# Entering the second part of three programs in the first instructions of a decode attention kernel

## The chip, the cores and the metric

The kernel runs on one core of a Trainium2 chip. A core has five engines that run programs of their own: TensorE (PE, matrix products; its weight loads are shown as PEld), VectorE (DVE), ScalarE (ACT), GpSimd (POOL) and SyncE (SP). Engines wait for one another through semaphores. Data moves between the chip's main memory (HBM) and the core's working memory (SBUF) by transfers that 16 DMA engines carry out; the engines' own program code is fetched by the same DMA engines, on queues that the profile calls "instruction". The metric is the device time of one execution in microseconds (us).

## The reference

One decode step of attention, 16 heads, one query row for each, 8192 keys of 256 numbers, all in bf16:

```python
B, H, Sq, Sk, D = 1, 16, 1, 8192, 256
scale = q.shape[-1] ** -0.5
scores = jnp.einsum("bhqd,bhkd->bhqk", q, k) * scale
p = _softmax(scores, axis=-1)
return jnp.einsum("bhqk,bhkd->bhqd", p, v)
```

K and V are 67 MB each and each of their numbers is used once.

## The kernel before, in words

The program of each engine is written out by hand; no scheduler moves anything. The keys of a head lie as 128 partitions of 64 keys, so a head's K is a buffer of 128 x 16384 bf16 numbers (4.19 MB) and its 64 columns of 256 numbers each hold 128 keys. There are two K buffers and two V buffers, used by even and odd heads.

**SP** (line 136) issues all K and V transfers in one order, the list `stream` of line 57: the first 16 columns of K of head 0, the other 48, K of head 1, half of V of head 0, K of head 2, the other half of V of head 0, half of V of head 1, and so on, with K two heads ahead of V. K of head h waits until VectorE and TensorE are done with head h-2 in that buffer (lines 132, 133), V until the weighted sum of head h-2 is done (line 135). All transfers go through one queue.

**DVE** computes the scores of the first 48 columns of a head: one multiply-and-sum for each column (line 189, two instructions), then the maximum over the head's 64 columns (line 206). It runs a loop of eight turns with an even and an odd head in each; the loop is one body of 213 instructions.

**PE** computes the other 16 columns: it transposes four K columns at a time (`ktrans`, line 278), ACT copies the result to SBUF (`evac`, line 367), and PE multiplies by q (`kscore`, line 292). It also combines the maximum across partitions (lines 226, 232), and makes the weighted sum of V (`pv`, line 257, 64 matmuls a head). Before its loop it spreads q over the partitions (lines 314 to 338). Its loop has nine turns: turn i computes the scores of heads 2i and 2i+1 and the weighted sums of heads 2i-2 and 2i-1, in the order scores, `pv`, scores, `pv`; turn 0 has no `pv` and turn 8 no scores, and conditional branches step over those parts.

**ACT** issues the load of q (line 401), copies the spread q out of PSUM (lines 404, 412), copies the q of the next head (line 362), evacuates the transposes, makes the exponentials (line 379), scales and stores the output rows (lines 392, 399).

What orders the work around the change is the programs' own order. DVE's program is 220 instructions as written, ACT's 83, PE's 599, with a matmul counted as two. DVE's loop begins at its instruction 4, ACT's loop at its instruction 18, PE's loop at its instruction 41.

Of the kernel before, what the change touches and what calls it, by code (L numbers as in the profile page):

```python
# [15 lines left out]
V_LATE = {14: (0, 16, 32, 48), 15: (0, 16, 32, 44, 52, 58, 62)}  # L16
AHEAD = {"kd": 1, "sc": 1, "sp": 2, "ex": 2, "m": 1, "g": 1, "mT": 1, "l": 1, "bc": 1, "nb": 1, "rc": 2, "pv": 2, "fin": 4}
V_SEMS = (("va0", "v0b", "v0c", "v0d"), ("va1", "v1b", "v1c", "v1d", "v1e", "v1f", "v1g"))
# [22 lines left out]
def bass_standalone__mha_softmax__decode_kernel(nc: bass.Bass, q: bass.AP, k: bass.AP, v: bass.AP, out: bass.AP):  # L41
    B, H, Sq, D = q.shape
    Sk = k.shape[2]
    P = 128
    J = Sk // P
    NH = D // P
# [24 lines left out]
    with contextlib.ExitStack() as ctx:  # L71
# [9 lines left out]
        def sem(name):  # L81
            if name not in sems:
                sems[name] = ctx.enter_context(nc.semaphore(name))
            return sems[name]
# [3 lines left out]
        q_sb = sb("q_sb", [H, D], dt)  # L88
# [5 lines left out]
        m = sb("m", [P, 2], FP32)  # L94
        g = sb("g", [1, 2], FP32)
# [4 lines left out]
        identb = sb("identb", [P, P], BF16)  # L100
# [8 lines left out]
        sm = ps("sm", [P, 512])  # L109
        qps = ps("qps", [P, 512])  # L110

        for name in ("pool", "cb", "cf", "qp", "qs", "qb", "kd", "tp", "kt", "sp", "sc", "m", "mT", "g", "bc", "nb", "ex"):
            sem(name)
        for name in ("l", "rc", "pv", "fin", "ldq", "k0", "k0b", "k1", "va0", "va1", "v1h", "o0", "o1"):
            sem(name)
# [1 line left out]
        for row in V_SEMS:  # L117
            for name in row[1:]:
                sem(name)

        def src(t, h):
            return t[0, h].rearrange("(p j) d -> p (j d)", p=P)

        if True:
# [44 lines left out]
            @(lambda f: f(nc.vector))  # L169
            def _(dve):  # L170
                def xmax(h):
                    dve.wait_ge(sem("mT"), h.of(1, 2))
                    dve.tensor_reduce(g[0:1, h.par : h.par + 1], mx[0:1, 0:P], AX.X, ALU.max).then_inc(sem("g"), 1)  # L173

                def recips(h):
                    dve.wait_ge(sem("l"), h.of(1, 2))
                    dve.wait_ge(sem("fin"), h.of(1, 3))
                    dve.reciprocal(recip[0:1, h.par : h.par + 1], qps[0:1, 0:1]).then_inc(sem("rc"), 1)  # L178

                def head(h, at):  # L180
                    dve.wait_ge(sem("qb"), h.of(1, 1))
                    dve.wait_ge(sem("ex"), h.of(1, 1))
                    dve.wait_ge(sem(f"k{h.par}"), h.of(8, 16 - 8 * h.par))
                    buf = kbuf[h.par]
                    for j in range(JD):
                        if j == K_FIRST and h.par == 0:

                            dve.wait_ge(sem("k0b"), 16)
                        ins = dve.tensor_tensor_reduce(  # L189
                            out=buf[:, j * D : (j + 1) * D],  # L190
                            in0=buf[:, j * D : (j + 1) * D],
                            in1=q_now[h.par][:, 0:D],
                            scale=SCALE,
                            scalar=0.0,
                            op0=ALU.mult,
                            op1=ALU.add,
                            accum_out=S[h.par][:, j : j + 1],
                        )
                        if j in at:
                            at[j]()  # L200
                    ins.then_inc(sem("kd"), 1)
                    if JD in at:
                        at[JD]()
                    dve.wait_ge(sem("kd"), h.of(1, 2))
                    dve.wait_ge(sem("sc"), h.of(1, 2))
                    dve.tensor_reduce(m[:, h.par : h.par + 1], S[h.par][:, :], AX.X, ALU.max).then_inc(sem("m"), 1)  # L206

                with dve.Fori(0, H // 2) as i:
                    ev, od = _Step(0, i), _Step(1, i)
                    prev = od.back(2)  # L210

                    def later(f):
                        with dve.If(i > 0):
                            f(prev)

                    head(ev, {40: lambda: later(xmax)})
                    head(od, {2: lambda: later(recips), 3: lambda: xmax(ev), JD: lambda: recips(ev)})
                last = _Step(H - 1)
                xmax(last)
                recips(last)  # L220

            @(lambda f: f(nc.tensor))
            def _(pe):
                def transpose_m(h):
                    pe.wait_ge(sem("m"), h.of(1, 2))
                    pe.matmul(  # L226
                        mx[0:1, 0:P], lhsT=m[:, h.par : h.par + 1], rhs=ident[:, :], start=True, stop=True
                    ).then_inc(sem("mT"), 1)
# [21 lines left out]
                def pv(h, waits, at):  # L250

                    pe.wait_ge(sem("fin"), h.of(1, 3))
                    pe.wait_ge(sem(f"va{h.par}"), h.of(8, 32 - 8 * h.par))
                    for j in range(J):
                        for name, value in waits.get(j, ()):
                            pe.wait_ge(sem(name), value)
                        ins = pe.matmul(  # L257
                            acc[h.par][0:1, 0:D],
                            lhsT=E[h.par][:, j : j + 1],
                            rhs=vbuf[h.par][:, j * D : (j + 1) * D],  # L260
                            start=(j == 0),
                            stop=(j == J - 1),
                        )
                        if j == J - 1:
                            ins.then_inc(sem("pv"), 1)
                        if j + 1 in at:
                            at[j + 1]()
# [33 lines left out]
                def scores(t, before=None):  # L301
                    if before:
                        transpose_m(before)
                    for gi in range(NG):
                        ktrans(t, gi)
                        if gi >= 1:
                            kscore(t, gi - 1)
                        if gi == 1 and before:
                            bcast(before)
                    kscore(t, NG - 1)  # L310
                    if before:
                        total(before)

                pe.wait_ge(sem("ldq"), 16)
                pe.wait_ge(sem("cb"), 1)
                for hf in range(NH):
                    ins = pe.matmul(
                        qps[:, hf * H : (hf + 1) * H],
                        lhsT=q_sb[:, hf * P : (hf + 1) * P],
                        rhs=identb[0:H, 0:H],  # L320
                        start=True,
                        stop=True,
                    )
                ins.then_inc(sem("qp"), 1)
                for h in range(H):
                    pair = h // 2
                    if h % 2 == 0 and pair >= 2:
                        pe.wait_ge(sem("qs"), pair - 1)
                    ins = pe.matmul(  # L329
                        acc[pair % 2][:, (h % 2) * D : (h % 2 + 1) * D],  # L330
                        lhsT=identb[0:H, h : h + 1].to_broadcast([H, P]),
                        rhs=q_sb[:, :],
                        start=True,
                        stop=True,
                    )
                    if h % 2 == 1:
                        ins.then_inc(sem("qp"), 1)
                pe.wait_ge(sem("cf"), 4)
                with pe.Fori(0, H // 2 + 1) as i:
                    ev, od = _Step(0, i), _Step(1, i)  # L340
                    fin_turn = pe.snap((i // 8) * 16 + 16)
                    half_turn = pe.snap(((i + 1) // 8) * 16 + 16)
                    old = od.back(2)
                    with pe.If(i < H // 2):
                        scores(ev)
                    with pe.If(i > 0):
                        pv(
                            ev.back(2),
                            {V_LATE[14][n]: [(V_SEMS[0][n], fin_turn)] for n in range(1, len(V_SEMS[0]))},
                            {32: lambda: transpose_m(old), 48: lambda: bcast(old), 64: lambda: total(old)},  # L350
                        )
                    with pe.If(i < H // 2):
                        scores(od, before=ev)
                    with pe.If(i > 0):
                        waits = {V_LATE[15][n]: [(V_SEMS[1][n], fin_turn)] for n in range(1, len(V_SEMS[1]))}
                        waits[HALF].append(("v1h", half_turn))
                        pv(old, waits, {})

            @(lambda f: f(nc.scalar))
            def _(act):  # L360
# [38 lines left out]
                    act.dma_start(dst, o_sb[h.par][0:1, :]).then_inc(sem(f"o{h.par}"), 16)  # L399

                act.dma_start(q_sb[:, :], q[0, :, 0, :]).then_inc(sem("ldq"), 16)
                by_head = q_all[:, 0 : H * QW].rearrange("p (h w) -> p h w", w=QW)
                act.wait_ge(sem("qp"), 1)
                act.activation(
# [75 lines left out]
```

## Time and profile before

| | |
|---|---|
| median of 3 runs | 320.71 us (320.42 to 320.89) |
| the profiled execution, whole | 321.04 us |
| its span, first to last instruction | 319.6 us |
| busy: DVE, PE, ACT | 274.9, 220.9, 92.0 us |
| moved by DMA | 134.29 MB, 420 GB/s over the span |
| instruction fetches | 5 packets, 0.05 MB |
| mean granted TensorE clock | 0.84 |

The page gives one profiled execution. Its parts are the busy time of each engine, the span in 40 slices with the granted clock and the DMA load, the DMA queues, the chain of work that ended last, the costliest groups of instructions and the DMA issues. Other views are tables of chosen stretches of time (windows), lists of instructions in order of time (timelines), the chain in order of time, and DMA queues within a stretch.

### The profile page before, as it was taken

Reading aid. Unit: us, or ns where it says so; the run is one execution under the profiler, and the core shown is the slowest. Engines: PE = TensorE matmul, PEld = TensorE weight load, DVE = VectorE, ACT = ScalarE, POOL = GpSimd, SP = SyncE. Lnnn points to the kernel's source line nnn. Section 1 sums busy time; section 2 is a strip of 40 time slices with the busy share of each in tenths; the row PEclk is TensorE's granted clock in tenths of the full one; section 3 lists DMA queues with packets and bytes.
Section 4 is the critical chain, followed back from the end, with each engine's and each line's share of the span. In section 5 each row is a group of like instructions: output and inputs, shape, how many; then the busy total and the mean of one; then the engine's idle time right before and its main releaser. Section 6 shows DMA issues by size and latency. Waiting matters only on the chain.

```text
span 319.6 us, 6845 instructions
## 1 busy us (share of the span) xinstructions
PE 220.9 (69%) x2162; PEld 156.3 (49%) x2162; DVE 274.9 (86%) x1584; ACT 92.0 (29%) x171; POOL 1.6 (0%) x11
## 2 busy tenths in 40 slices
PE   4427186797875947849297573966749477397997
PEld 1326154565554635626256352653626355265675
DVE  2799999999999998897979979889797997979910
ACT  5436050433224060510506123060231605116010
POOL 1000000000000000000000000000000000000000
PEclk9999999769598786969769598785969969587799
DMA  8999999999999999999999999999999999999994
GB/s 329 451 397 455 392 453 416 416 427 435 439 418 443 431 435 439 418 439 427 439 435 423 439 418 443 431 431 435 427 439 414 447 435 427 439 406 423 422 399 179
DMA packets 6549, 134.29 MB, mean 420 GB/s; under 512 B 752, under 2 KB 912, under 8 KB 1424
## 3 DMA queue, kind: packets, MB, share of 16 engines
q1 hardware_dynamic: 6480, 134.22, 98.3%
q8 instruction: 2, 0.03, 0.0%
q10 hardware_dynamic: 64, 0.02, 0.0%
q14 instruction: 3, 0.02, 0.0%
HBM read 134.23 MB, written 0.01 MB: 420 GB/s over the span
## 4 chain that ended last, share of the span: by engine, by line
DMA 49%; PE 24%; DVE 23%; issue 2%; ACT 1%; ACTq 0%; SPq 0%; DVEq 0%
DMA vbuf<-in_v_dram 45%; PE acc L257 23%; DVE kbuf L189 22%; DMA kbuf<-in_k_dram 4%; DVE S L189 1%; PE sm L232 1%; ACT KT L367 1%; PE mx L226 0%; ACT o_sb L392 0%; ACT q_now L362 0%; DVE g L173 0%; SPq L136 0%; PE spe L292 0%; ACTq L399 0%; DVE recip L178 0%
## 5 line engine op out<-in xcount | busy, mean ns | idle before, releaser
L189 DVE CUSTOM_DVE_ANT_0 kbuf<-kbuf,q_now 128x256 bf16<-128x256 bf16 x768 | 268.1, 413 | 22.2 <-DMA kbuf<-in_k_dram 21.2
L257 PE MATMUL acc<-vbuf,E 128*1 128x256 bf16 x1024 | 147.6, 315 | 36.3 <-DMA vbuf<-in_v_dram 36.3
L257 PEld LDWEIGHTS acc<-vbuf,E 128*1 128x1 bf16 x1024 | 96.7, 96 | 80.4 <-DMA vbuf<-in_v_dram 37.3
L367 ACT ACTIVATE KT<-tp 128x1024 bf16<-128x1024 bf16 x64 | 63.8, 1018 | 30.3 <-PE tp L278 30.1
L189 DVE DVE_READ_ACCUMULATOR2_ANT S<- 128x1 f32 x768 | 58.4, 76 | 0.0
L278 PE MATMUL tp<-identb,kbuf 128*128 128x128 bf16 x512 | 42.3, 239 | 13.9 <-DMA kbuf<-in_k_dram 13.8
L292 PE MATMUL spe<-q_now,KT 128*128 128x1 bf16 x512 | 23.1, 166 | 32.3 <-ACT KT L367 31.6
L278 PEld LDWEIGHTS tp<-identb,kbuf 128*128 128x128 bf16 x512 | 33.5, 107 | 18.3 <-DMA kbuf<-in_k_dram 12.4
L292 PEld LDWEIGHTS spe<-q_now,KT 128*128 128x128 bf16 x512 | 18.0, 100 | 42.0 <-ACT KT L367 32.0
L392 ACT ACTIVATE o_sb<-acc,recip 1x256 bf16<-1x256 f32 x16 | 7.4, 464 | 99.9 <-PE acc L257 98.6
L375 ACT ACTIVATE negb<-sm 128x1 f32<-128x1 f32 x16 | 2.8, 172 | 84.5 <-PE sm L232 84.5
L173 DVE TENSOR_REDUCE g<-mx 1x1 f32<-1x128 f32 x16 | 4.4, 276 | 9.8 <-PE mx L226 9.8
L226 PE MATMUL mx<-ident,m 128*1 128x128 f32 x32 | 6.3, 279 | 5.7 <-DVE m L206 5.7
L232 PE MATMUL sm<-g,ones_row 1*128 1x1 f32 x32 | 6.2, 262 | 4.1 <-DVE g L173 4.1
L232 PEld LDWEIGHTS sm<-g,ones_row 1*128 1x128 f32 x32 | 4.9, 190 | 6.2 <-DVE g L173 4.7
L362 ACT ACTIVATE q_now<-q_all 128x258 bf16 (+1 forms) x17 | 7.0, 412 | 0.3 <-DVE S L189 0.3
L178 DVE RECIPROCAL recip<-qps 1x1 f32<-1x1 f32 x16 | 2.4, 151 | 3.9 <-PE qps L242 3.9
L379 ACT ACTIVATE E<-S,negb 128x64 bf16<-128x64 f32 x16 | 5.6, 348 | 0.5
L226 PEld LDWEIGHTS mx<-ident,m 128*1 128x1 f32 x32 | 2.2, 83 | 6.3 <-DVE m L206 5.9
L329 PE MATMUL acc<-q_sb,identb 16*128 16x256 bf16 x16 | 4.4, 403 | 1.0 <-ACT q_all L412 1.0
L371 ACT ACTIVATE S<-spe 128x16 f32<-128x16 f32 x16 | 2.9, 183 | 7.3 <-PE spe L292 7.3
L412 ACT ACTIVATE q_all<-acc 128x512 bf16<-128x512 f32 x8 | 4.4, 593 | 0.9 <-PE acc L329 0.9
(20 smaller groups left out, 16.6 us busy)
## 6 DMA issues: line engine op xcount, KB each, us to landing
kbuf<-in_k_dram SPq DMA_DIRECT2D x15, 4096.0 KB, 20.5
vbuf<-in_v_dram SPq DMA_DIRECT2D x11, 4096.0 KB, 29.0
vbuf<-in_v_dram SPq DMA_DIRECT2D x6, 2048.0 KB, 24.4
vbuf<-in_v_dram SPq DMA_DIRECT2D x6, 1024.0 KB, 12.8
kbuf<-in_k_dram SPq DMA_DIRECT2D x1, 3072.0 KB, 11.7
kbuf<-in_k_dram SPq DMA_DIRECT2D x1, 1024.0 KB, 4.8
vbuf<-in_v_dram SPq DMA_DIRECT2D x1, 768.0 KB, 9.1
vbuf<-in_v_dram SPq DMA_DIRECT2D x1, 512.0 KB, 9.9
```

The source lines that it names most:

```text
L173: dve.tensor_reduce(g[0:1, h.par : h.par + 1], mx[0:1, 0:P], AX.X, ALU.max).then_inc(sem("g"), 1)
L189: ins = dve.tensor_tensor_reduce(out=buf[:, j * D : (j + 1) * D], in0=buf[:, j * D : (j + 1) * D], in1=q_now[h.par][:, 0:D], scale=SCALE, ...
L226: pe.matmul(mx[0:1, 0:P], lhsT=m[:, h.par : h.par + 1], rhs=ident[:, :], start=True, stop=True).then_inc(sem("mT"), 1)
L232: pe.matmul(sm[:, 0:1], lhsT=ones_row[0:1, 0:P], rhs=g[0:1, h.par : h.par + 1], start=True, stop=True,).then_inc(sem("bc"), 1)
L257: ins = pe.matmul(acc[h.par][0:1, 0:D], lhsT=E[h.par][:, j : j + 1], rhs=vbuf[h.par][:, j * D : (j + 1) * D], start=(j == 0), stop=(j == J ...
L278: ins = pe.transpose(tp[gi % 2][:, b * D + hf * P : b * D + (hf + 1) * P], buf[:, j * D + hf * P : j * D + (hf + 1) * P], identb[:, :],)
L292: ins = pe.matmul(spe[:, c : c + 1], lhsT=KT[gi % 2][:, b * D + hf * P : b * D + (hf + 1) * P], rhs=q_now[h.par][:, D + hf : D + hf + 1], ...
L329: ins = pe.matmul(acc[pair % 2][:, (h % 2) * D : (h % 2 + 1) * D], lhsT=identb[0:H, h : h + 1].to_broadcast([H, P]), rhs=q_sb[:, :], start ...
L362: act.activation(out=q_now[h.par][:, :], in_=src_q, func=ACT.Copy).then_inc(sem("qb"), 1)
L367: act.activation(out=KT[gi % 2][:, :], in_=tp[gi % 2][:, :], func=ACT.Copy).then_inc(sem("kt"), 1)
L379: act.activation(out=E[h.par][:, :], in_=S[h.par][:, :], func=ACT.Exp, bias=negb[:, h.par : h.par + 1], scale=1.0, accum_out=lsum[:, h.par ...
L392: act.activation(out=o_sb[h.par][0:1, :], in_=acc[h.par][0:1, 0:D], func=ACT.Copy, scale=recip[0:1, h.par : h.par + 1],).then_inc(sem("fin ...
```

## The change: an early visit to later code

TensorE, VectorE and ScalarE each execute, in their first instructions, a jump to code that lies further on in their program. For VectorE and ScalarE a new helper writes an `If` that is never taken around 50 and 66 no-operations, so that the engine jumps over them; the code behind is moved on by as many instructions. VectorE's helper stands ahead of its loop, ScalarE's behind the issue of the q load. For TensorE no padding is used: the first half of the loop's body is put in an inner loop, which has one empty turn (r = 0) in turn 0 of the outer loop, so that the program runs to the inner loop's end and back again; in all other turns of the outer loop the inner one begins at r = 1 and runs once. The spreading of q, formerly ahead of the loop, becomes the first part of that inner body and is done in turn 0. The work, its order on each engine and its waits are the same.

```diff
+        def skip_ahead(eng, n):
+
+            zero = eng.alloc_register(f"zero_{n}_{eng.engine.value}")
+            eng.reg_mov(zero, 0)
+            with eng.If_ne(zero, 0):
+                for _ in range(n):
+                    eng.nop().then_inc(sem("pad"), 1)
...
+                skip_ahead(dve, 50)
                 with dve.Fori(0, H // 2) as i:
...
-                pe.wait_ge(sem("ldq"), 16)
-                pe.wait_ge(sem("cb"), 1)
...
+                def spread_q():
+                    pe.wait_ge(sem("ldq"), 16)
+                    pe.wait_ge(sem("cb"), 1)
...
                 with pe.Fori(0, H // 2 + 1) as i:
...
-                    with pe.If(i < H // 2):
-                        scores(ev)
-                    with pe.If(i > 0):
-                        pv(
...
+                    with pe.Fori(pe.snap((i + 8) // 9), 2) as r:
+                        with pe.If(r > 0):
+                            with pe.If(i == 0):
+                                spread_q()
+                            with pe.If(i < H // 2):
+                                scores(ev)
+                            with pe.If(i > 0):
+                                pv(
...
                     with pe.If(i < H // 2):
                         scores(od, before=ev)
...
                 act.dma_start(q_sb[:, :], q[0, :, 0, :]).then_inc(sem("ldq"), 16)
+                skip_ahead(act, 66)
```

More of the change, by code (lines that the diff above doesn't have):

```diff
@@ L110, in bass_standalone__mha_softmax__decode_kernel @@
         qps = ps("qps", [P, 512])
-        for name in ("pool", "cb", "cf", "qp", "qs", "qb", "kd", "tp", "kt", "sp", "sc", "m", "mT", "g", "bc", "nb", "ex"):
+        for name in ("pad", "pool", "cb", "cf", "qp", "qs", "qb", "kd", "tp", "kt", "sp", "sc", "m", "mT", "g", "bc", "nb", "ex"):
             sem(name)
@@ L312, in scores @@
                         total(before)
-                pe.wait_ge(sem("ldq"), 16)
-                pe.wait_ge(sem("cb"), 1)
[L316 to L337, printed above, removed]
@@ L338, in _ @@
-                pe.wait_ge(sem("cf"), 4)
+                def spread_q():
+                    pe.wait_ge(sem("ldq"), 16)
+                    pe.wait_ge(sem("cb"), 1)
+                    for hf in range(NH):
+                        ins = pe.matmul(
+                            qps[:, hf * H : (hf + 1) * H],
+                            lhsT=q_sb[:, hf * P : (hf + 1) * P],
+                            rhs=identb[0:H, 0:H],
+                            start=True,
+                            stop=True,
+                        )
+                    ins.then_inc(sem("qp"), 1)
+                    for h in range(H):
+                        pair = h // 2
+                        if h % 2 == 0 and pair >= 2:
+                            pe.wait_ge(sem("qs"), pair - 1)
+                        ins = pe.matmul(
+                            acc[pair % 2][:, (h % 2) * D : (h % 2 + 1) * D],
+                            lhsT=identb[0:H, h : h + 1].to_broadcast([H, P]),
+                            rhs=q_sb[:, :],
+                            start=True,
+                            stop=True,
+                        )
+                        if h % 2 == 1:
+                            ins.then_inc(sem("qp"), 1)
+                    pe.wait_ge(sem("cf"), 4)
@@ L343, in _ @@
                     old = od.back(2)
-                    with pe.If(i < H // 2):
-                        scores(ev)
-                    with pe.If(i > 0):
-                        pv(
[L348 to L351, printed above, removed]
+                    with pe.Fori(pe.snap((i + 8) // 9), 2) as r:
[6 more added lines that the diff above has]
+                                pv(
+                                    ev.back(2),
+                                    {V_LATE[14][n]: [(V_SEMS[0][n], fin_turn)] for n in range(1, len(V_SEMS[0]))},
+                                    {32: lambda: transpose_m(old), 48: lambda: bcast(old), 64: lambda: total(old)},
+                                )
                     with pe.If(i < H // 2):
```

## The prediction

> **What bounds the kernel now.** I read the page's shares and DMA queues first, then the chain that ended last, then windows and timelines of the first 64 us, where all that the change touches lies.
>
> ```profile
> span 319.6 us, 6845 instructions
> ...
> PE 220.9 (69%) x2162; PEld 156.3 (49%) x2162; DVE 274.9 (86%) x1584; ACT 92.0 (29%) x171; POOL 1.6 (0%) x11
> ...
> q1 hardware_dynamic: 6480, 134.22, 98.3%
> q8 instruction: 2, 0.03, 0.0%
> ...
> q14 instruction: 3, 0.02, 0.0%
> ```
>
> K and V, 134.22 MB on queue q1, fill the 16 DMA engines 98.3% of the span; no other resource is near that. Program code is only 5 packets.
>
> The chain in order of time shows what sets the end:
>
> ```profile
> 247.26 29.66 DMA vbuf<-in_v_dram
> ...
> 276.97 6.03 PE acc L257 x32
> ...
> 293.47 13.27 PE acc L257 x96
> ...
> 310.88 7.02 PE acc L257 x64
> 317.98 0.47 ACT o_sb L392
> ```
>
> Up to 276.92 us (247.26 + 29.66, V of head 12) it is the transfers; from there some 41 us of PE, without a break in the last 24. So the end moves with the landing of V 12, and with anything that lengthens PE's last turns. The stretches that matter for the stream are these windows (the last column is GB/s):
>
> ```profile
> 0.00:8.00 8.00, 3.49 (x16) 1.10 (x16) 2.37 (x13) 4.63 (x9) 1.56 (x11) 1.00 0.83 329
> ...
> 16.00:24.00 8.00, 2.29 (x36) 1.73 (x34) 8.00 (x48) 2.49 (x4) 0.00 (x0) 1.00 0.93 396
> ...
> 32.00:40.00 8.00, 1.06 (x11) 1.07 (x12) 8.00 (x49) 0.00 (x0) 0.00 (x0) 1.00 0.93 395
> ...
> 80.00:280.00 200.00, 137.31 (x1378) 96.60 (x1376) 181.36 (x1047) 54.88 (x103) 0.00 (x0) 0.79 1.00 432
> ```
>
> A head's K or V is 134.22/32 = 4.19 MB. V 12 is the 28th of these, 117.4 MB. With 329 GB/s x 8 us = 2.63 MB in the first window and 432 GB/s afterwards it would be through at 8 + 114.8/0.432 = 273.8 us. It lands at 276.92. So all that is lost between 8 us and V 12 is 3.1 us: no edit in the early part can win more.
>
> **What the change moves: code fetches.** The DMA queues, asked by stretch: first 0 to 4 us, then 17 to 18, 22 to 23.5, 32 to 33.5, 33.5 to 36.5 and 36.5 to 38 us (the share is of 16 DMA engines over the stretch).
>
> ```profile
> q1 hardware_dynamic: 87, 0.71, 53.1%
> q10 hardware_dynamic: 32, 0.01, 1.5%
> ...
> q14 instruction: 1, 0.01, 1.9%
> ...
> q8 instruction: 1, 0.02, 4.2%
> ...
> q14 instruction: 1, 0.01, 1.3%
> ...
> q8 instruction: 1, 0.02, 2.1%
> ...
> q14 instruction: 1, 0.01, 1.4%
> ```
>
> No code comes in the first 4 us and none after 38; all five packets come in turn 0, inside the K and V stream. Times of one DMA engine: 1.9% x 16 x 1 us = 0.30, 4.2% x 16 x 1.5 = 1.01, 0.31, 1.01, 0.34 us; 2.97 in all. I take the two large q8 packets for PE, whose program is by far the longest, and the q14 ones for DVE and ACT. None of them stops an engine: DVE is busy 8.00 of 8.00 us in both windows in which they fall, and ACT and PE wait there for other things:
>
> ```profile
> 18.69 0.38 PE L292 MATMUL spe<-q_now,KT 128*128 128x1 bf16 x8 [0.77 <-ACT KT L367]
> 24.33 0.59 PE L226 MATMUL mx<-ident,m 128*1 128x128 f32 x2 [5.26 <-DVE m L206]
> ```
>
> PE ends its first stretch at 19.07 and begins again at 24.33, released by DVE's maximum; the packet of 22 to 23.5 us is through by then. So as a removed stall the change is worth nothing. [...]
>
> What is left is on whose back the packets travel.
>
> *Won later.* If the jumps bring fetches forward, I count one for each engine: 1.01 (PE) + 0.30 (DVE) + 0.31 (ACT) = 1.62 us of single DMA engines leave the stream between 17 and 34 us. PE's second half and the end of DVE's loop lie further on than the places jumped to, so 1.01 and 0.34 stay. A transfer has landed when its last sixteenth has. So the win at V 12 is between 0 (the engine that is last is one that keeps its packet) and 1.62 (all three sit on the last one). I take 0.3: a packet of 1.01 stays, and the worst engine before can hardly have carried much more than 1.01 + 0.3.
>
> *Paid at the start.* The moved packets now meet the first K transfers. What depends on those:
>
> ```profile
> 0.73 1.32 SPq L136 DMA_DIRECT2D kbuf<-in_k_dram  x3
> ...
> 5.63 0.43 DVE L189 CUSTOM_DVE_ANT_0 kbuf<-kbuf,q_now 128x256 bf16<-128x256 bf16 x1 [5.63 <-DMA kbuf<-in_k_dram]
> ...
> 12.86 0.42 DVE L189 CUSTOM_DVE_ANT_0 kbuf<-kbuf,q_now 128x256 bf16<-128x256 bf16 x1 [1.61 <-DMA kbuf<-in_k_dram]
> ...
> 24.05 0.33 SPq L136 DMA_DIRECT2D kbuf<-in_k_dram  x1
> ...
> 58.73 0.33 SPq L136 DMA_DIRECT2D kbuf<-in_k_dram  x1
> ```
>
> DVE's start at 5.63 has 1.61 us of room, because after 16 columns it waits for the other 48 of K 0, to 12.86. That second landing has none: DVE runs on from it almost without a pause, and its ends of heads 0 and 2 issue K 2 (24.05) and K 4 (58.73). The queue ahead of K 2 is K 0, K 1 and half of V 0, 10.49 MB, empty at 8 + 7.86/0.432 = 26.2 us; ahead of K 4 it is 25.17 MB, empty at 60.2. So K 4 is issued 1.4 us before its turn, K 2 2.1 us. Is that enough? The windows behind it:
>
> ```profile
> 61.00:62.00 1.00, 0.45 (x9) 0.28 (x5) 1.00 (x7) 0.34 (x1) 0.00 (x0) 1.00 0.67 246
> 62.00:63.00 1.00, 0.26 (x8) 0.26 (x8) 1.00 (x7) 1.00 (x3) 0.00 (x0) 1.00 0.76 311
> ```
>
> It is not: 0.67 and 0.76 of the DMA engines busy, 246 and 311 GB/s. So whatever delays the second part of K 0 delays K 4's issue and widens this hole. The price is between 0 (the packets pass before the K data, whose first issue ends at about 1.1 us) and 1.62 (all on the last engine); PE's alone is 1.01. I take 0.6: PE's request can't be early in its queue, as the q8 packet of turn 0 came 3 us or more after PE ran out of its first stretch (19.07 to 22 at least), and 3 us after PE's first instructions is in the middle of K 0; a part of it will lie on an engine that was not last. DVE's and ACT's 0.30 I count as hidden by the spread between DMA engines; uncovered they would make it 0.9.
>
> *Control instructions.* DVE gets a register set and a branch at 0.7 us, and waits to 5.63: nothing. ACT gets the same ahead of its table load:
>
> ```profile
> 0.73 0.41 ACTq L401 DMA_DIRECT2D q_sb<-in_q_dram  x1
> 1.18 1.28 ACT L404 ACT_TABLE_LOAD   x1 [1.18 <-PEq L465]
> 3.96 0.20 ACT L404 ACTIVATE q_all<-qps 128x32 bf16<-128x32 f32 x1 [1.50 <-PE qps L317]
> ```
>
> ACT waits 1.50 us for PE there, and DVE's 1.61 stand behind it: nothing. PE gets about eight register and branch instructions a turn. For one of them I have ACT's rows of the chain:
>
> ```profile
> 287.84 0.03 issue
> 287.87 0.03 ACTq L399
> 287.89 0.03 issue
> ```
>
> At 0.03 + 0.03 that is 0.5 us a turn on PE's sequencer. It counts only in the last two turns, and there it is covered: the piece at 293.47, 96 matmuls without a gap, contains the loop's present back edge and two branches. Nothing; without that cover up to 0.5 in each of two turns, 1.0. POOL and SP are not edited, and no instruction moves past another on any queue.
>
> **Sum.** -0.3 + 0.6 = +0.3 us on the profiled execution's 321.04 (a span of 319.6 and 1.4 around it), which is 0.33 above the median; on the median it is 321.0.
>
> **Rivals.**
> - *A clean win.* The early packets cost nothing, and the engine that is last loses more than I take, up to 1.62; midway 0.9, so 319.8. For it: no data moves until after 0.73. Against it: two of five packets stay, and PE's come late.
> - *K 0's second part is late (slower).* Both PE's and DVE's packet fall on the last engine: 1.01 + 0.30 = 1.3, less 0.3 won, +1.0: 321.7. It decides from a delay of DVE's start at 12.86 of over 0.94 us (0.64 + 0.3). For it: the hole at 61 us shows that there is no reserve. Against it: 16 engines, few packets.
> - *The jump itself stalls.* [...] The bound is PE's 19.07 to the end of the 23.5 us stretch, 4.4 us. ACT would go on at 1.14 + 4.4 = 5.54, end the table load at 6.8 and be 2.9 late at its first activation; less DVE's 1.61 that is 1.25, with 0.3 won +0.95: 321.7. It decides from a stall of over 4.1 us. Against it: in turn 0 before, each engine ran into new code and none waited for it. [...] No row here shows such a stall.
> - *Nothing moves.* The packets come where they came: 320.7.
>
> **How the numbers follow.** Chances: my sum (321.0, its own range 320.4 to 321.3) 0.32; nothing moves 0.12; clean win 0.22; K 0 late 0.24; stalled jump 0.10. A measurement of this kernel tells about 0.2%, 0.64 us, from no change. So faster 0.22, same 0.44, slower 0.34. The range of 8 in 10 cuts off about the outer half of the clean win, and the upper end of the two slow cases: 319.8 to 321.9.
>
> **What would show it.** In the profile after: instruction packets in the first 4 us, three fewer between 17 and 34, and one of q8 size and one of q14 size left between 24 and 38. If no packet comes early, nothing moved. DVE's row now at 12.86 tells the price at the start, and K 4's issue, now 58.73, must move with it; the windows at 61 to 63 us show the hole narrower or wider. The first ACT row after the table load, now 3.96, later than about 7 would be the stalled jump. V 12's landing, now 276.92, must carry the whole difference, and the 41 us of PE behind it stay as they are. I am wrong if the difference arises behind 276.92, or if K 0 lands as before and the stream gains over 0.6.

## The result, and the profile after

The changed kernel takes 321.81 us at the median of 20 runs (320.20 to 323.37), the kernel before 320.59 us (320.12 to 321.98): a ratio of 1.0034, 95% interval 1.002 to 1.0048. That is 1.1 us slower by the ratio, 1.2 us by the medians. The runs of the changed kernel scatter more: 13 of 20 are above 321.5 us, and 5 of 20 of the kernel before.

The page of the profile after shows the same work and the same five packets of code:

```profile
span 320.4 us, 6899 instructions
...
q1 hardware_dynamic: 6480, 134.22, 98.2%
q8 instruction: 2, 0.03, 0.0%
...
q14 instruction: 3, 0.02, 0.0%
```

The DMA queues of the changed kernel, asked for 4.5 to 5.3, 5.3 to 7 and 10 to 11 us (q1 carries K and V, the other queues code; the last number is the share of 16 engines over the stretch):

```profile
q1 hardware_dynamic: 47, 0.49, 144.3%
q8 instruction: 1, 0.02, 7.3%
...
q14 instruction: 1, 0.01, 1.2%
...
q14 instruction: 1, 0.01, 1.9%
```

Three packets have moved from between 17 and 34 us to between 5 and 11, into the transfers of K 0: 7.3% x 16 x 0.8 = 0.93 us of one DMA engine for the large one, 0.33 and 0.30 for the others. One of each size stays, at 37 and 33 us. What this does is seen in the timelines of VectorE (first column, and column 16, the first one of K 0's second part) and of SP's issues (K 2 and K 4):

```profile
5.84 0.42 DVE L197 CUSTOM_DVE_ANT_0 kbuf<-kbuf,q_now 128x256 bf16<-128x256 bf16 x1 [5.84 <-DMA kbuf<-in_k_dram]
14.25 0.43 DVE L197 CUSTOM_DVE_ANT_0 kbuf<-kbuf,q_now 128x256 bf16<-128x256 bf16 x1 [2.79 <-DMA kbuf<-in_k_dram]
...
25.44 0.33 SPq L144 DMA_DIRECT2D kbuf<-in_k_dram  x1
...
60.12 0.33 SPq L144 DMA_DIRECT2D kbuf<-in_k_dram  x1
```

VectorE's start is 0.21 later, which its room covers. But the second part of K 0 comes 1.39 us later (14.25 for 12.86), and K 2 and K 4 are issued 1.39 us later, one for one. The end of the chain, in order of time:

```profile
249.99 28.40 DMA vbuf<-in_v_dram
...
278.43 5.63 PE acc L266 x32
...
311.74 7.02 PE acc L266 x64
...
318.84 0.47 ACT o_sb L407
```

V 12 lands at 278.39 in place of 276.92, 1.47 us later, and PE's first products of V 12 begin 0.04 us behind it, as before. The span grows by less, 0.8 us; PE's part behind V 12 is 0.6 us shorter here, and the last section comes back to that.

### The profile page after: what moved, and what is told of

The parts are those of the page before. It is cut to its first block, busy times and chain, and to the rows that moved or that the text cites. A ratio compares the mean times of both kernels' runs of the same rounds, so it can differ in the third digit from the quotient of the medians.

```text
span 320.4 us, 6899 instructions
## 1 busy us (share of the span) xinstructions
PE 222.7 (69%) x2162; PEld 157.2 (49%) x2162; DVE 274.9 (86%) x1584; ACT 91.9 (29%) x171; POOL 1.6 (0%) x11
## 4 chain that ended last, share of the span: by engine, by line
DMA 48%; PE 25%; DVE 23%; issue 2%; ACT 1%; ACTq 0%; SPq 0%; DVEq 0%
DMA vbuf<-in_v_dram 44%; PE acc L266 23%; DVE kbuf L197 22%; DMA kbuf<-in_k_dram 4%; DVE S L197 1%; PE sm L241 1%; ACT KT L382 1%; PE mx L235 0%; ACT o_sb L407 0%; ACT q_now L377 0%; DVE g L181 0%; SPq L144 0%; PE spe L301 0%; ACTq L414 0%; DVE recip L186 0%
```

## The experiments

The theory that I took into the runs (A): a code packet that falls into K 0's transfers delays K 0's second part; VectorE runs on from it later, K 2 and K 4 are issued later, and the stream gets a longer hole. The rivals: (B) the new branches cost TensorE time; (C) the packets themselves, or the DMA engine that carries them and is behind afterwards, are the cost, whatever VectorE does.

**Which part of the change.** The first kernel has TensorE's empty turn alone; these two lines of the changed kernel are out:

```diff
-                skip_ahead(dve, 50)
-                skip_ahead(act, 66)
```

> TensorE's empty turn alone; VectorE and ScalarE as before. Theory A (a code fetch that falls into K 0's transfers delays the landing of K 0's second part, VectorE runs on from it later, K 2 and K 4 are issued later, the stream has a longer hole): a packet of about 16 KB between 2 and 12 us, VectorE goes on with column 16 at 13.5 to 14.3 us in place of 12.86, K 4 is issued as much later, and the time is 0.2% to 0.4% above the kernel before. Theory B (the new branches cost TensorE time at its loop's turns): the same rise, but VectorE at 12.86 as before and the difference behind the landing of V 12. Theory C (the small packets of the two other engines do it): no change.

Ratio 1.000 (0.998 to 1.002). Its queues at 4.5 to 5.3 us and its VectorE:

```profile
q8 instruction: 1, 0.02, 7.3%
```

```profile
14.27 0.43 DVE L197 CUSTOM_DVE_ANT_0 kbuf<-kbuf,q_now 128x256 bf16<-128x256 bf16 x1 [2.62 <-DMA kbuf<-in_k_dram]
```

So the q8 packets are TensorE's, and its early packet alone delays K 0's second part by 1.41 us, as much as the whole change. That is more than the packet's own 0.93 us. In the trace's packet records the data packet that begins as the code packet ends (5.97) takes 1.42 us, where others of its size take 0.91; if it is the same engine's, as the times suggest, that engine is 0.93 + 0.51 = 1.44 us behind.

Yet the median does not rise, against the 0.2% to 0.4% that theory A expected. This is the first sign that the delay does not become time one for one.

The second kernel has the padding of VectorE and ScalarE on the kernel before, and no inner loop.

> The padding of VectorE and ScalarE alone; TensorE as before. Theory A: two packets of 8 KB in the first 12 us, each 0.3 us of one DMA engine, so VectorE goes on at column 16 at most 0.7 us later (12.9 to 13.5), and the time is 0 to 0.2% above the kernel before. Theory B: no change at all. Theory C: all of the 0.34% of the whole change.

Ratio 1.0012 (0.9996 to 1.0027). Two q14 packets come, at 5.7 and 10.4 us, and the large one stays at 24:

```profile
13.60 0.43 DVE L197 CUSTOM_DVE_ANT_0 kbuf<-kbuf,q_now 128x256 bf16<-128x256 bf16 x1 [2.13 <-DMA kbuf<-in_k_dram]
```

The two small packets delay K 0 by 0.74 us. The data packet behind the second of them takes 1.49 us in place of 0.91, so a small packet, too, costs more than its own 0.31. Neither half alone can be told from no change in 12 runs.

The third has TensorE's inner loop and all its branches without the empty turn:

```diff
-                    with pe.Fori(pe.snap((i + 8) // 9), 2) as r:
+                    with pe.Fori(pe.snap((i + 9) // 9), 2) as r:
```

> TensorE's inner loop with all its branches, but without the empty turn (it starts at r = 1 in turn 0 too), so no early visit; VectorE and ScalarE as before. Theory A: the time of the kernel before (within 0.1%), the first packet of code after 15 us, VectorE at column 16 at 12.86. Theory B: the rise of 0.3% stays.

Ratio 1.000 (0.998 to 1.002); no packet of code from 2 to 17 us, VectorE at column 16 at 13.09, V 12 at 276.90. Rival B is out.

**The delay without the code.** VectorE of the kernel before is held back by memsets (instructions that fill an unused buffer with zeros), so that K 2 and K 4 are issued late while no code comes early:

```diff
+        idle = sb("idle", [P, 11 * D], FP32)
...
+                dve.wait_ge(sem("qb"), 1)
+                for w in range(11):
+                    dve.memset(idle[:, w * D : (w + 1) * D], 0.0)
                 with dve.Fori(0, H // 2) as i:
```

> The kernel before, with eleven memsets of 128 x 256 numbers in VectorE's program behind its wait for the first q and ahead of its loop, so that its first column starts some 2.5 to 3.5 us later. No code fetch is moved into K 0. Theory A: room is 1.61 us, so what is beyond it (about 1 to 2 us) goes to the issues of K 2 and K 4 one for one, V 12 lands later by nearly as much and the time rises by 0.6 to 0.9 of it, 0.2% to 0.5%. A theory that the fetched bytes themselves or the lag of the DMA engine that carries them make the kernel slower: no change (within 0.1%).

Ratio 1.000 (0.998 to 1.002). The memsets took 3.01 us, and the issues stand where the changed kernel has them:

```profile
25.37 0.33 SPq L137 DMA_DIRECT2D kbuf<-in_k_dram  x1
...
60.05 0.33 SPq L137 DMA_DIRECT2D kbuf<-in_k_dram  x1
```

But V 12 lands at 276.91, as in the kernel before. Theory A, which expected 0.2% to 0.5%, falls in this form: 1.3 us of later issue, alone, has no cost that 12 runs show.

This gives a second theory (A2). The 16 DMA engines reach the end of the queue at different times, because some have carried code: the 16 landing events that the trace has for K 0's second part, one for each sixteenth (I take each for one engine's), lie between 12.35 and 12.84 us in the kernel before, ahead of its first code, and between 12.32 and 14.23 in the changed one, behind three packets of it. A short hole stops those that come first, and they have time to spare: V 12 has landed only when the last one is through (its events run from 275.02 to 276.92 us before, and PE's first product of V 12 begins at 276.97). A hole costs time only where it falls on an engine that is already last; that is the theory, for the next runs to decide.

With 26 memsets in place of 11:

> The kernel before with 26 memsets (about 7.1 us) ahead of VectorE's loop, so column 16 starts about 5.5 us later than before and K 2 is issued at about 29.5 us, 3.3 us behind the end of the queue. Theory A2: now every DMA engine stands empty, those that are behind too, so the time rises: 5.5 us less the reserve of 2.1 us, less the 0.6 to 1.5 us by which the last engine is behind, plus up to 2 us for the start of a transfer: +1.5 to +4 us. If the issues of K 2 and K 4 did not matter at all: no change, as with eleven memsets.

Ratio 1.0138 (1.010 to 1.018) in 4 runs, 4.4 us, somewhat over the 1.5 to 4 us expected. K 2 is issued at 29.40; the windows show the DMA engines empty (second number from the right):

```profile
28.00:29.00 1.00, 0.00 (x0) 0.00 (x0) 1.00 (x7) 0.00 (x0) 0.00 (x0) 1.00 0.00 0
29.00:30.00 1.00, 0.32 (x2) 0.09 (x2) 0.96 (x8) 0.00 (x0) 0.00 (x0) 1.00 0.00 0
```

So the issues do count once the hole reaches every DMA engine, as A2 says. No run shows the "up to 2 us for the start of a transfer" in the expectation's sum. What is on record is that the first packet of K 0 starts at 1.74 us in the kernel before, 1.0 after its issue at 0.73, and that none of K 2 starts before 30.0 here, 0.6 after its issue at 29.40.

**Taking the reserve's limit away.** K 0 comes in three pieces, so that VectorE need not wait at column 16:

```diff
-stream = [("k", 0, 0, K_FIRST, "k0"), ("k", 0, K_FIRST, J, "k0b"), ("k", 1, 0, J, "k1")]
+stream = [("k", 0, 0, K_FIRST, "k0"), ("k", 0, K_FIRST, K_NEXT, "k0m"), ("k", 0, K_NEXT, J, "k0b"), ("k", 1, 0, J, "k1")]
...
                         if j == K_FIRST and h.par == 0:
+                            dve.wait_ge(sem("k0m"), 16)
+                        if j == K_NEXT and h.par == 0:
                             dve.wait_ge(sem("k0b"), 16)
```

Here K_NEXT is 32. First on the kernel before:

> The kernel before, with K 0 in three pieces (16, 16 and 32 columns) in place of two, so that VectorE need not wait at column 16: K 2 and K 4 are then issued some 1.6 us earlier (about 22.4 and 57.1). Theory A2 (a hole at K 2 or K 4 costs time when it falls on a DMA engine that is already behind by its code fetches; it hits engines by chance): no hole, DMA engines busy in every stretch from 24 to 66 us, the slowest executions go, median 320.2 to 320.5, the spread of the runs under 1 us. Rival (the lag of the engine that carries the code is all there is): median as before, within 0.1%.

Then on the changed kernel:

> The changed kernel with K 0 in the same three pieces; the early code fetches stay. Theory A2: the change costs nothing any more, within 0.1% of the other kernel with three pieces, because the pieces that VectorE needs next have several us of room. Rival: the 0.34% of the change stays.

Ratios to the kernel before: 0.9989 (0.997 to 1.0005) without the change, 0.9992 (0.9975 to 1.0008) with it. In the second, the code still comes at 5.0, 5.4 and 10.4 us, but K 2 is issued early again, and K 4 (58.73 before) is no longer late:

```profile
22.85 0.33 SPq L145 DMA_DIRECT2D kbuf<-in_k_dram  x1
...
58.65 0.33 SPq L145 DMA_DIRECT2D kbuf<-in_k_dram  x1
```

With room at K 0 the change costs nothing that 12 runs show. So the packets by themselves (rival C) are not the cost. Three parts of what I had expected without the change are misses. The median is 320.73, not 320.2 to 320.5, and the runs spread over 1.35 us, not under 1. K 4 is issued only 0.7 us earlier than before (58.01 without the change), since VectorE then waits for K 1 (1.11 us, to 23.48). The hole at 61 us is gone all the same. The windows show 0.80 of the DMA engines busy at 61 to 63 us, but they count a packet's whole time where it starts, and show 1.56 at 60 to 61. By the landing events K 4 follows the transfer ahead of it 9.7 us later from the first sixteenth to the last, as the 22 transfers of this size behind K 4 do in the kernel before (9.71 to 9.73 us from first event to first event).

**The same kernels again.**

> The changed kernel once more, beside the others on the same chip: 0.2% to 0.5% above the kernel before, with the code fetches again within the first 12 us, and K 2 and K 4 issued 0.7 to 1.5 us later than before.

> The changed kernel a third time: 0.1% to 0.4% above the kernel before. Theory A2: the first packets of code again at about 5, 5.5 and 10.3 us, VectorE at column 16 at 14.1 to 14.3, K 2 issued at 25.3 to 25.4; V 12 at 276.9 where the hole spares the last DMA engine, at 278 or later where it falls on it.

> The kernel before, run as a kernel of its own, for a second profile and a measure of what two equal kernels differ by: ratio 1 within 0.15%. Theory A2: if its profile shows the holes at K 2 or K 4 on a DMA engine that was already last, V 12 lands at 277.5 us or later and the run is over 321.4; if not, V 12 lands at 276.9.

> The kernel before with K 0 in three pieces once more, to narrow its ratio: theory A2 expects 0.05% to 0.2% under the kernel before, and no run above 321.6.

Ratios: the changed kernel 1.0012 (0.9993 to 1.003) and 1.0039 (1.002 to 1.006); the kernel before against itself 1.0000 (0.998 to 1.002); three pieces 0.9999 (0.998 to 1.001). Three expectations were missed: the first repeat of the changed kernel lies below its 0.2% to 0.5%; three pieces are not 0.05% to 0.2% faster; and the second profile of the kernel before, with V 12 at 277.29 in a run of 320.64, fits neither of the two cases named. The three profiles of the changed kernel have the same early packets and the same late issues, and differ in when K 2 and K 4 have landed. The last number of these rows of the DMA issues is the time from issue to landing of K 4; the changed kernel's three profiles, then the one with 11 memsets:

```profile
kbuf<-in_k_dram SPq DMA_DIRECT2D x1, 4096.0 KB, 14.3
```

```profile
kbuf<-in_k_dram SPq DMA_DIRECT2D x1, 4096.0 KB, 13.0
```

```profile
kbuf<-in_k_dram SPq DMA_DIRECT2D x1, 4096.0 KB, 13.0
```

```profile
kbuf<-in_k_dram SPq DMA_DIRECT2D x1, 4096.0 KB, 12.9
```

All profiles together (us from the start; landing of K 4 is its issue plus the time to landing, and V 12's likewise):

| kernel | column 16 | K 2 issued | K 4 issued | K 4 landed | V 12 landed | span |
|---|---|---|---|---|---|---|
| before | 12.86 | 24.05 | 58.73 | 72.93 | 276.92 | 319.6 |
| before, second profile | 12.93 | 24.11 | 58.80 | 73.30 | 277.29 | 319.2 |
| changed | 14.25 | 25.44 | 60.12 | 74.42 | 278.39 | 320.4 |
| changed, second | 14.09 | 25.27 | 59.96 | 72.96 | 276.95 | 319.6 |
| changed, third | 14.09 | 25.27 | 59.95 | 72.95 | 276.97 | 318.8 |
| TensorE alone | 14.27 | 25.45 | 60.13 | 73.33 | 277.78 | 320.4 |
| VectorE, ScalarE alone | 13.60 | 24.79 | 59.47 | 74.47 | 278.33 | 321.7 |
| inner loop, no empty turn | 13.09 | 24.27 | 58.95 | 72.85 | 276.90 | 320.0 |
| 11 memsets | 14.25 | 25.37 | 60.05 | 72.95 | 276.91 | 320.0 |
| 26 memsets | 18.4 | 29.40 | 64.09 | 77.99 | 282.11 | 324.9 |
| three pieces | no wait | 22.14 | 58.01 | 72.91 | 276.98 | 319.2 |
| three pieces, changed | no wait | 22.85 | 58.65 | 72.95 | 276.89 | 319.6 |
| three pieces, second profile | no wait | 22.44 | 57.94 | 72.84 | 276.87 | 319.1 |
| three pieces, long jump (below) | no wait | 22.63 | 59.06 | 73.16 | 277.17 | 319.0 |

(Column 16 with memsets is the first column's start, 8.72 with 11 of them, and 16 columns of 0.346 us; with 26 it is worked out the same way.) V 12 lands 203.9 to 204.5 us after K 4 in every row: nothing behind K 4 matters to the stream here. K 4 itself lands at 72.8 to 73.0 in eight of the fourteen.

The landing events bear A2 out. With three pieces the first sixteenth of K 4 lands at 70.86 and the last at 72.95; with 11 memsets at 71.73 and 72.91. So the holes cost the first engine 0.9 us and the last one nothing. They also show where the holes are. On the mean of the 16, K 4 comes 0.3 to 0.5 us later than the 9.7 in the kernel before, and just as much in the changed one. What the change adds is at K 2: there it is 0.2 in the kernel before, as with three pieces (two packets of code fall there in each), and 0.4 to 0.6 in the changed kernel and with 11 memsets.

Where a row is late, the last engine has lost time at K 2 or at K 4. From last sixteenth to last sixteenth, K 2 takes 11.4 us in the changed kernel's first profile, 10.0 and 10.2 in its second and third, and 10.3 with 11 memsets, although it is issued as late there. With VectorE's and ScalarE's padding alone K 2 takes 10.3, but K 4 takes 11.2. No code is near that one: it is a hole that reached the last engine. At K 2 of the first profile the two late packets of code, at 33 and 37 us, are a rival to the hole; the second and third have theirs in the same transfer, and which engine carried them is not on record.

How often an execution is slow shows in the single runs. Above 321.5 us were 29 of 131 runs of the kernel before (22%), 25 of 44 of the changed kernel (57%), 2 of 36 with K 0 in three pieces, changed or not (6%), and 4 of 12 with 11 memsets. In the three comparisons of the changed kernel it was 13 of 20 against 5 of 20, 5 of 12 against 7 of 29, and 7 of 12 against 2 of 35. The parts of the change and the 11 memsets were compared with a kernel before that had 11 of 35: TensorE alone 3 of 12, VectorE and ScalarE alone 5 of 12. A run without a profile does not tell where its time went.

**A long jump.** The last run puts a jump over 600 no-operations into TensorE's program, ahead of its loop, on the kernel with three pieces.

```diff
+                skip_ahead(pe, 600)
                 with pe.Fori(0, H // 2 + 1) as i:
```

> [...] The stalled jump of the prediction: TensorE's first transposes come later than the landing of K 0 (over 13.5 us in place of about 13.0), by up to 4 us, and a packet of code is seen between the jump (about 9 us) and them. Since K 2 has room here, theory A2 expects a time within 0.1% of the kernel with three pieces, unless one more packet of code lies on the DMA engine that is last (then up to 1 us more).

Ratio 1.0003 (0.999 to 1.002). TensorE's timeline, and the queues at 12 to 13.5 us:

```profile
8.70 0.60 PE L339 MATMUL acc<-q_sb,identb 16*128 16x256 bf16 x2 [0.20 <-ACT q_all L423]
15.61 1.86 PE L288 MATMUL tp<-identb,kbuf 128*128 128x128 bf16 x16 [6.30 <-DMA kbuf<-in_k_dram]
```

```profile
q8 instruction: 1, 0.02, 4.4%
```

Without the long jump the first transposes start at 12.80; here at 15.61, 2.8 us later, with a packet of code at 12.6 in between. Not all of that is the jump's: K 0's last piece, which they need, lands 13.0 us after its issue at 1.63, at about 14.6; without the long jump 11.0 us after it, at about 12.6 (the rows of the two kernels):

```profile
kbuf<-in_k_dram SPq DMA_DIRECT2D x1, 2048.0 KB, 13.0
```

```profile
kbuf<-in_k_dram SPq DMA_DIRECT2D x1, 2048.0 KB, 11.0
```

But the trace's record of the jump's own branch instruction, which waits for no data, runs from 8.80 to 15.02, 6.2 us; the branch in its place without the long jump takes 0.09. This is the stalled jump. In the changed kernel it does not occur: no branch of the three engines takes over 0.4 us. TensorE's first matmul is at 3.92 and ScalarE's first activation at 4.17, 0.21 later than before, both behind the landing of q.

## Why the prediction was right or wrong

- *What bounds the kernel, and that no stall is removed.* Right. The end went with V 12, and VectorE, TensorE and ScalarE had not waited for code: no branch of theirs in the kernel before takes over 0.4 us.
- *What moves.* Right in number and size: three packets forward, one of each size left. Wrong in the time of its sign: I looked for them in the first 4 us; they came at 5.0, 5.9 and 10.3. The price had put TensorE's in the middle of K 0, and that is where it fell.
- *Won later, 0.3.* Not found. Where nothing falls on the last engine, K 4 and V 12 land at 72.95 and 276.95 in the changed kernel and 72.93 and 276.92 before: 0.
- *Paid at the start, 0.6.* The term that was mis-sized, and not by size alone. The delay of K 0's second part is 1.39 us, near the upper bound of 1.62. The price of one packet was too low: TensorE's, put at no more than 1.01, makes 1.41 alone, as the data packet behind it is slow too (1.42 for 0.91). I had counted the small packets as hidden; alone they make 0.74. The issues of K 2 and K 4 followed one for one, as the step said. But the step took every delay there as a wider hole at K 4, paid in full. The hole at K 4 is no wider than before, 0.4 to 0.5 us on the mean engine (the 0.67 and 0.76 of the windows are partly due to the 1.74 in the window ahead of them); the new hole is at K 2, for which I had counted 2.1 us of reserve. The 11 memsets make the same delay for nothing, and two of three profiles of the changed kernel lose nothing at V 12 either. What measured 1.1 us is a median over executions of which more are slow, 57% against 22% above 321.5.
- *Control instructions, nothing.* Right (inner loop without the empty turn: 1.000).
- *The rivals.* The case that occurred is the slower one, K 0's second part late, and its 321.7 is the measured time; my own sum, 321.0, was given more chance and is 0.8 short. The sign was right, and the time lies in the range, 0.1 below its upper end. That 321.7 fits so well is partly luck: its working charges the late landing to every execution, and two of three profiles do not pay it. The stalled jump occurred with the jump over 600 no-operations (6.2 us), where the prediction had no row that showed one, and not in this change (0.4 us at most).
- *"V 12's landing must carry the whole difference, and the 41 us of PE behind it stay."* Half right, and in the first profile only. V 12 carried 1.47 us; the part behind it went from 42.7 to 42.1. In the other two V 12 stayed, and that part was 42.6 and 41.8.

What stays open: 11 memsets and the changed kernel delay the issues alike, and only the latter is measurably slower (1.000, 0.998 to 1.002, against 1.0034, 1.002 to 1.0048; the intervals just touch). That early code puts more engines behind, so that a hole meets a last one more often, is argued and not shown. The landing events lend it little: at the end of the transfer ahead of K 2, one or two of 16 engines are over 1 us behind the first in the kernel before, and two or three in the changed one. TensorE alone, as late as the whole change, was not slower. And the part behind V 12 differs by up to 1.5 us between profiles, for a reason of its own (see the end), as much as the cost itself. No profile of the changed kernel is of a run above 321.9 us, so where its slowest runs, up to 323.5, lose their time is not on record.

## What to carry to other kernels

Code that comes ahead of need can delay the data: here TensorE's early 16 KB packet alone made K 0's second part 1.41 us late. Look for a place where the landing that it delays has slack: with K 0 in three pieces the same early code cost nothing that 12 runs show (0.9992), the first 12 us of the kernel before had no such slack, and in the two stretches where the code came before VectorE was busy without a pause (8.00 of 8.00 us). Ask of a stream that is "98% busy" how early each transfer is issued before its turn (here K 2 and K 4 met no hole in any profile where they were issued 2.6 us or more before the first engine had finished the transfer ahead, and at 2.5 us or less they met one in all cases but one), and which of the 16 engines finishes last: delays shorter than the gap between first and last engine may be free, as the 1.3 us of later issue with 11 memsets were (1.000; the gap at the end of the transfer ahead of K 2 is 1.7 us in the kernel before). Where a cost comes only in some executions, one profile of each kernel can show the opposite of the median (the third profile of the changed kernel has the shortest span of the table, 318.8), so count runs as well.

## What the runs showed of the hardware that I had not expected

The code packets came late. In the changed kernel's first profile the jumps of VectorE and ScalarE run at 0.83 and 1.24 us, TensorE's from 1.23 to 1.99; the packets come at 5.0, 5.9 and 10.3, the large one first, and within 0.5 us of that in the other two. When each was asked for is not on record.

And a packet cost more than its own time: 0.93 us and 0.51 more at the next data packet for 16 KB, 0.31 and 0.58 more for the second of the 8 KB ones in the run of VectorE's and ScalarE's padding.

The span behind V 12's landing varies from 41.8 to 43.4 us with the same matrix products, and goes with when the granted clock of TensorE is halved (the trace's clock records hold 1.0 and 0.5 in turn, in the kernel before 0.5 at 271.6 to 281.9 and 292.1 to 298.9 us): over the 14 profiles, half clock takes 6.2 to 12.7 of the first 30 us behind V 12, and the longer it lasts, the longer this part is, within 0.1 us. The windows of 282 to 287 and 297 to 302 us in the changed kernel's third profile (span 318.8, clock third from the right):

```profile
282.00:287.00 5.00, 4.64 (x46) 3.35 (x44) 3.12 (x17) 1.08 (x4) 0.00 (x0) 1.00 0.96 410
...
297.00:302.00 5.00, 5.00 (x48) 3.84 (x47) 5.00 (x31) 0.47 (x1) 0.00 (x0) 1.00 1.01 419
```

and in that of VectorE's and ScalarE's padding alone (span 321.7):

```profile
282.00:287.00 5.00, 5.00 (x36) 3.38 (x34) 2.82 (x16) 0.00 (x0) 0.00 (x0) 0.78 0.98 419
...
297.00:302.00 5.00, 5.00 (x28) 3.09 (x27) 5.00 (x29) 0.00 (x0) 0.00 (x0) 0.57 1.01 419
```

1.00 against 0.78 and 0.57. The part behind V 12 is 41.8 us in the one and 43.4 in the other, over half of the 2.9 us between the two spans; the rest is V 12's landing, 276.97 against 278.33. In the first of the two the chain's end runs through the last transfer of V, landed at 311.34, so that a higher clock alone would not shorten it further.
